# Block-sparse attention with an MLP on one Trainium2 core: the row of maxima written by ScalarE in twelve heads, and one pair of heads fewer multiplied in whole fp32

## The chip, the cores and the metric

The kernel runs on one core of one Trainium2 chip. The metric is the device time of one execution in microseconds (us), the median of three runs. The engines are named as in the profile: PE is TensorE's matmul and PEld its weight load, DVE is VectorE, ACT is ScalarE, POOL is GpSimd, SP is SyncE, which here only issues DMAs.

## What is computed

Four batches of eight heads, 768 positions, head dimension 64. Scores are masked by blocks of 32 (neighbours, first and last block, and three drawn blocks for each row of blocks), and an MLP with a piecewise activation follows on the joined heads:

```python
scores = scale * np.matmul(q, k.transpose(0, 1, 3, 2))
scores = np.where(mask, scores, -1000000000.0)
scores = scores - np.max(scores, axis=-1, keepdims=True)
attn = np.exp(scores)
attn = attn / (np.sum(attn, axis=-1, keepdims=True) + 1e-09)
attn_out = np.matmul(attn, v)
...
h = x @ w_in
g = np.where(pos, h, np.where(neg, 0.0, (h + beta) ** 2 / (4.0 * beta)))
return (g @ w_out).astype(np.float32)
```

## The kernel before

**Accuracy by splitting.** Most matmuls run in the type F32R. To keep fp32 accuracy an operand is split into a rounded part and a remainder, and products of the parts are added up. Queries and keys of a head lie in QA and KA (rounded parts, rows 0 to 63, and below them the mask rows 64 to 95) and in QB and KB (remainders beside rounded parts). There are two sets of QA and KA, used by heads in turn (SETS is 2).

**A head**, `head` (L198), works in this order. Twelve matmuls `max_mm` (L267) give the masked scores by rows, and twelve DVE reductions `max_red` (L272) their row maxima. `max_col` (L276) joins the two halves of each maximum into the tile mr, 128 x 6. `max_turn` (L280) transposes mr on PE into 6 x 128 in a PSUM bank. `max_row` (L283), on DVE, multiplies it by a constant of minus ones on a diagonal and so writes six rows of QA, 96 to 101; the keys have six rows of ones there, so that the matmul of the scores subtracts the maximum. Then, for each of two halves of the queries and six blocks of keys, `scores` (L303, L304: two F32R matmuls of 384 columns), `expo` (L308, ACT), and `values` (L333 to L336).

**Whole and split heads.** For the pairs of heads in WHOLE, which are heads 0 to 9, `values` is one fp32 matmul with the exponentials as they are (L333); ones beside the values give the row sums, and `o_whole` (L351, L353) copies both out on ACT. For all other heads ACT rounds each exponential (`p_hi`, the helper's line L196), DVE subtracts (`p_lo`, L316), PE multiplies twice (L335, L336), POOL adds the exponentials up (`p_sum`, L323), DVE reduces that sum (L358), adds two halves of the output (L345, after a copy by ACT on L340), and splits the values of the head (L243). A small matmul (L363) and L369 give the sums of a pair.

**Wide heads.** Heads 0 to 7 (batch 0) have no MLP work beside them; they may use the MLP's PSUM banks for scores, and the three `pa` banks are left to the maxima. From head 8 on, the scores, the maxima and the transposed maxima all share the three `pa` banks, and the MLP of the batch before (`moe`, L434: L457 to L459, L463 to L478, L485 to L487) runs between the heads' steps. Its first half, beside heads 8 to 11, also makes the two parts of w_out out of float64 bits (`convert`, L157; DVE lines L169 to L180, ACT L168 and L196). The same is done with w_in beside heads 0 to 7.

**Order.** Each step is put on a list with a due time (`at`, L129) worked out from the constants P, PW (wide heads) and PA (heads 8 to 15); the list is sorted and given to the framework, which puts in the waits. An engine works through its own instructions in order. None of these due times is touched by the change. All DMAs but one small kind are issued by SP.

Of the kernel before, what the change touches and what calls it, by code (L numbers as in the profile page):

```python
# [9 lines left out]
F32R = mybir.dt.float32r  # L10
# [10 lines left out]
T = 6  # L21
HALF = 384
# [15 lines left out]
def body(ctx, tc, qk_t, v, sampled_blocks, moe_w_in, moe_w_out, ind, cm, negd, ident, fold, out):  # L38
    nc = tc.nc
# [8 lines left out]
    pr = pool("pr", 1)  # L48
# [24 lines left out]
    def f(ap):  # L73
        return ap.bitcast(F32)


    idr = cst.tile([128, 128], F32R, name="idr")
# [4 lines left out]
    QA = [cst.tile([128, S], F32R, name=f"QA{i}") for i in range(SETS)]  # L82
# [4 lines left out]
    def consts():  # L87
        M = slice(64, KM)
        for i in range(SETS):
            nc.gpsimd.memset(f(QA[i][64:128 if i == 0 else 96]), 0.0)  # L90
        nc.gpsimd.memset(VW[0][:, :, 64:128], 1.0)
        nc.gpsimd.memset(VW[1][:, :, 0:64], 1.0)
        nc.vector.memset(eps, 1e-9)
        nc.vector.memset(half_c, 0.5)
        sraw = cst.tile([128, NR, 2], I32, name="sraw")
        nc.sync.dma_start(out=sraw[M], in_=sampled_blocks.bitcast(I32).rearrange("a (r w) -> a r w", w=2))
        cmt = cst.tile([128, 2 * NB], F32, name="cmt")
        nc.sync.dma_start(out=cmt[M], in_=cm)
        ef = f(cv.tile([128, 512, 2], I32, name="raw", bufs=3).rearrange("p c w -> p (c w)"))[64:KA, 0:S]
        nc.sync.dma_start(out=ef, in_=ind)  # L100
        idf = pp.tile([128, HALF], F32, name="pt")[:, 0:128]
        nc.sync.dma_start(out=idf, in_=ident)
        nc.vector.tensor_copy(out=idr, in_=idf)
        nc.vector.tensor_copy(out=KAt[0][64:KA], in_=ef)
        nc.sync.dma_start(out=nd, in_=negd.rearrange("a (t p) -> a t p", t=T))
        nc.sync.dma_start(out=sel, in_=fold)
        for i in range(1, SETS):
            rounded(nc.gpsimd, KAt[i][64:KA], ef)
        sf = cst.tile([128, NR], F32, name="sf")
        nc.vector.tensor_copy(out=sf[M], in_=sraw[M, :, 0])  # L110
        al = cst.tile([128, NB], F32, name="al")
        nc.vector.tensor_copy(out=al[M], in_=cmt[M, 0:NB])
        for r in range(NR):
            nc.vector.scalar_tensor_tensor(
                out=al[M], in0=cmt[M, NB:2 * NB], scalar=sf[M, r:r + 1], in1=al[M],
                op0=ALU.is_equal, op1=ALU.max)
        mb = cst.tile([128, NB], F32R, name="mb")
        nc.vector.tensor_scalar(out=mb[M], in0=al[M], scalar1=-1.0, scalar2=BIG, op0=ALU.add, op1=ALU.mult)
        for hf in range(2):
            cs = slice(hf * HALF, (hf + 1) * HALF)  # L120
            pm = psa.tile([128, 512], F32, name="pa")
            nc.tensor.matmul(out=pm[0:NB, 0:HALF], lhsT=mb[M], rhs=KAt[0][64:KM, cs], start=True, stop=True)
            for i in range(SETS):
                (nc.scalar.copy if i else nc.vector.tensor_copy)(out=QA[i][64:KM, cs], in_=pm[0:NB, 0:HALF])
# [4 lines left out]
    def at(t, fn, *args):  # L129
        plan.append((t, fn, args))  # L130
# [3 lines left out]
    def bank(wide, use="s"):  # L134

        if wide:
            ring = RINGS[use]
            n = turns[use] = turns.get(use, -1) + 1
            name = ring[n % len(ring)]
            if name[0] == "o":  # L140
                return psc.tile([128, DM], F32, name=name)
            if name == "hp":
                return psh.tile([128, 512], F32, name="hp")
        return psa.tile([128, 512], F32, name="pa")
# [45 lines left out]
    def rounded(eng, dst, src):  # L190
        if eng is nc.vector:
            eng.tensor_copy(out=dst, in_=src)
        elif eng is nc.gpsimd:
            eng.tensor_scalar(out=dst, in0=src, scalar1=1.0, scalar2=0.0, op0=ALU.mult, op1=ALU.add)
        else:
            eng.copy(out=dst, in_=src)  # L196

    def head(i, n0, b, h, pst):  # L198

        j, e = divmod(h, 2)  # L200
        wide = i < H
        whole = i // 2 in WHOLE
        G = {**P, **PW} if wide else {**P, **PA} if i < 2 * H else P
        o0, o1 = (L, R) if e == 0 else (R, L)
        QAi, KAi = QA[i % SETS], KAt[i % SETS]
        st = {}
# [67 lines left out]
        def max_col(lo=0, n=T):  # L274
            mr = st["mr"] = pr.tile([128, T], F32R, name="mr", bufs=2)
            nc.vector.tensor_tensor(out=mr[:, 0:n], in0=st["mc"][:, 0:n, 0], in1=st["mc"][:, 0:n, 1], op=ALU.max)  # L276

        def max_turn(lo=0, n=T):
            pm = st["pr"] = bank(wide, "m")
            nc.tensor.transpose(out=pm[0:n, 0:128].bitcast(F32R), in_=st["mr"][:, 0:n], identity=idr)  # L280

        def max_row(lo=0, n=T):
            nc.vector.tensor_tensor(out=QAi[96:96 + n].rearrange("a (t p) -> a t p", t=T)[:, lo:n],  # L283
                                    in0=st["pr"][0:n, 0:128].unsqueeze(1).to_broadcast([n, n - lo, 128]),
                                    in1=nd[0:n, lo:n], op=ALU.mult)
# [6 lines left out]
        if i == 0:  # L292
            for d, fn in ((-0.9, max_col), (-0.89, max_turn), (-0.88, max_row)):
                at(pre - (G["m0"] - G["m1"] / 2) + G["mr"] + H0 + d, fn, 0, T // 2)
        at(pre - G["mc"], max_col, T // 2 if i == 0 else 0)
        at(pre - G["mt"], max_turn, T // 2 if i == 0 else 0)
        at(pre - G["mw"], max_row, T // 2 if i == 0 else 0)


# [98 lines left out]
        for hf in range(2):  # L398
# [19 lines left out]
            if e:  # L418
# [6 lines left out]
                y -= G["r1"]  # L425
                y += G["r2"] + (XLATE if wide and j < NP - 1 else 0)
                at(y + G["xm"], x_mul, hf)
# [98 lines left out]


    at(TC, consts)
    for i in range(NHEADS):
        b, h = divmod(i, H)  # L530
        if h % 2 == 0:
            pst = {}
        head(i, PER * i, b, h, pst)
# [17 lines left out]
        fn(*args)  # L551


WHOLE = (0, 1, 2, 3, 4)
P = {'vw': 4.0, 'r1': 0.857, 'r2': 4.031, 'qs': 9.647, 'ks': 11.666, 'vs': 9.131, 'ld': 5, 'm0': 7.832, 'm1': 5.0, 'mr': 0.46, 'mc': 2.3, 'mt': 1.325, 'mw': 0.9, 'ex': 0.524, 'ph': 1.22, 'pl': 1.349, 'ps': 0.841, 'ow': 0.704, 'ot': 0.2, 'oa': 0.549, 'ah': 0.3, 'al': 0.578, 'su': 0.637, 'de': 1.414, 'yw': 0.799, 'yy': 2.173, 'xm': 0.774, 'xh': 1.0, 'xl': 2.518, 'gr': 0.1, 'gs': 0.279, 'gm': 0.314, 'gh': 0.934, 'gl': 1.232, 'l2': 1.494, 'l3': 0.158, 'l1': 0.121, 'cl': 9.0, 'cs': 1.705, 'cd': 1.8, 'co': 5.196, 'lag': 3.5}
PW = {'vw': 4.0, 'r1': 3.302, 'r2': 4.413, 'qs': 12.454, 'vs': 9.131, 'ld': 5, 'm0': 7.8, 'm1': 5.61, 'mr': 0.15, 'mc': 2.3, 'mt': 1.3, 'mw': 0.9, 'ex': 0.2, 'ph': 1.231, 'pl': 1.349, 'ps': 0.841, 'ow': 0.722, 'ot': 0.2, 'oa': 0.462, 'ah': 0.3, 'al': 0.578, 'su': 0.637, 'de': 1.525, 'yw': 0.813, 'yy': 2.024, 'xm': 0.516, 'xh': 1.1600000000000001, 'xl': 2.268, 'lag': 3.403}
TC = -90
XLATE = 2.0
H0 = 0.711
PH1 = ()  # L560
# [67 lines left out]
```

## Time and profile before

| | us |
|---|---|
| median of 3 runs | 982.35 (981.95 to 989.32) |
| the profiled execution, its own time | 983.67 |
| its span, first to last instruction | 981.8 |
| PE busy | 942.5 |
| DVE busy | 747.5 |
| ACT busy | 636.5 |
| POOL busy | 251.8 |

The profiled execution's own time is 1.9 us over its span, and 1.3 us over the median. The first exponential (L308) of head 8 starts at 151.1 us, that of head 10 at 206.1 and that of head 12 at 274.4, so that the stretch 17 to 151 is heads 0 to 7, 151 to 206 is heads 8 and 9, and 206 to 274 is heads 10 and 11. In a row of groups the two numbers behind the first bar are busy us and mean ns of one instruction; behind the second bar is the idle time of the engine just before them and what ended most of it. Durations of successive instructions overlap a little, so that a group's sum may exceed what it adds to the engine's busy time.

### The profile page before, as it was taken

To read this page: it belongs to the slowest core of one execution; us is meant where nothing else is said; L and a number is where in the kernel's file an instruction comes from. 1 tells how busy PE (TensorE), PEld (TensorE's weight loads), DVE (VectorE), ACT (ScalarE), POOL (GpSimd) and SP (SyncE) were. 2 spreads that over 40 slices of the span, in tenths; PEclk is the share of its full clock that TensorE was granted. 3 is DMA by queue.
4 is the path that set the end of the run, shared out by engine and by line. 5 is a ranking of instruction groups with operands and counts; after the bars stand their busy time and mean duration, and the time that the engine had idled before them with its cause. 6 is when DMAs were issued, how large, how long until landed. Compare 5 with 4: busy or idle time off the path is not lost.

```text
span 981.8 us, 14556 instructions
## 1 busy us (share of the span) xinstructions
PE 942.5 (96%) x4687; PEld 828.1 (84%) x4687; DVE 747.5 (76%) x1403; ACT 636.5 (65%) x1302; POOL 251.8 (26%) x229
## 2 busy tenths in 40 slices
PE   5899899999889999999999999999999999999998
PEld 3666677877779899999989998998999999899997
DVE  5888999889998888978788888888888885422222
ACT  3667777677667676767677767776767676433433
POOL 1000000023334343433434343343434343000000
PEclk9999999999999999999999999999999999999999
DMA  6756677754355444645555443645445432433432
GB/s 195 205 149 189 196 209 225 259 180 139 123 182 163 145 143 133 182 139 153 159 150 182 131 150 116 199 137 175 138 142 178 125 115 89 154 130 129 160 129 97
DMA packets 56216, 154.43 MB, mean 157 GB/s; under 512 B 9612, under 2 KB 17952, under 8 KB 56140
## 3 DMA queue, kind: packets, MB, share of 16 engines
q1 hardware_dynamic: 56100, 153.48, 51.5%
q8 instruction: 37, 0.61, 0.3%
q14 instruction: 39, 0.32, 0.1%
q10 hardware_dynamic: 40, 0.03, 0.0%
HBM read 100.92 MB, written 14.81 MB: 118 GB/s over the span
## 4 chain that ended last, share of the span: by engine, by line
PE 85%; DVE 7%; ACT 3%; DMA 2%; issue 2%; SPq 0%; ACTq 0%; DVEq 0%
PE oa L485 8%; PE oa L487 8%; PE oa L486 8%; PE hp L457 8%; PE hp L459 7%; PE hp L458 7%; PE pa L267 7%; PE pa L303 5%; PE pa L304 5%; PE po L335 5%; PE po L336 4%; PE po L333 4%; DVE mc L272 2%; PE oa L333 2%; DMA QA<-qkh 1%
## 5 line engine op out<-in xcount | busy, mean ns | idle before, releaser
L323 POOL TENSOR_TENSOR acc<-acc,pt 128x384 f32<-128x384 f32 x176 | 201.7, 1146 | 233.0 <-ACT pt L308 195.1
L272 DVE TENSOR_REDUCE mc<-pa 128x1 f32<-128x384 f32 x384 | 202.5, 547 | 19.3 <-PE pa L267 16.1
L196 ACT CAST ph<-pt 128x384 fp32r<-128x384 f32 x264 | 135.5, 514 | 92.4 <-PE po L335 89.3
L316 DVE TENSOR_TENSOR pl<-pt,ph 128x384 fp32r<-128x384 f32 x264 | 163.6, 620 | 34.7 <-ACT ph L196 34.0
L308 ACT ACTIVATE pt<-pa 128x384 f32<-128x384 f32 x288 | 140.6, 489 | 54.6 <-PE pa L304 45.0
L457 PE MATMUL hp<-x,wi 128*128 128x384 f32 x448 | 155.5, 347 | 4.0 <-DVE r L469 4.0
L485 PE MATMUL oa<-w,gh 128*128 128x512 f32 x384 | 153.3, 399 | 0.3 <-ACT gh L196 0.3
L487 PE MATMUL oa<-w,gl 128*128 128x512 f32 x384 | 151.6, 395 | 0.3 <-DVE gl L478 0.3
L459 PE MATMUL hp<-x,wi 128*128 128x384 f32 x448 | 151.2, 338 | 0.0
L458 PE MATMUL hp<-x,wi 128*128 128x384 f32 x448 | 151.1, 337 | 0.0
L486 PE MATMUL oa<-w,gh 128*128 128x512 f32 x384 | 150.8, 393 | 0.0
L267 PE MATMUL pa<-KA,QA 88*128 88x384 f32 x384 | 138.3, 380 | 5.4 <-DMA QA<-qkh 3.8
L323 POOL TENSOR_TENSOR acc<-pt 128x384 f32<-128x384 f32 x44 | 46.5, 1058 | 345.5 <-ACT pt L308 345.5
L469 DVE SCALAR_TENSOR_TENSOR r<-r,hp 128x384 f32<-128x384 f32 x112 | 61.5, 549 | 73.3 <-ACT r L466 72.9
L478 DVE TENSOR_TENSOR gl<-r,gh 128x384 fp32r<-128x384 f32 x128 | 84.3, 658 | 24.0 <-ACT gh L196 23.5
L303 PE MATMUL pa<-QA,KA 102*128 102x384 f32 x288 | 99.0, 344 | 1.8 <-ACT pt L308 1.1
L463 ACT ACTIVATE r<-hp,half_c 128x384 f32<-128x384 f32 x112 | 65.1, 582 | 54.1 <-PE hp L459 51.2
L304 PE MATMUL pa<-QB,KB 128*128 128x384 f32 x288 | 97.9, 340 | 0.0
L267 PEld LDWEIGHTS pa<-KA,QA 88*128 88x128 f32 x384 | 73.1, 192 | 28.7 <-DVE mc L272 4.7
L335 PE MATMUL po<-ph,vn 128*128 128x384 f32 x264 | 91.4, 346 | 5.1 <-DVE xun L345 3.4
L457 PEld LDWEIGHTS hp<-x,wi 128*128 128x128 f32 x448 | 84.5, 189 | 10.7 <-DVE r L469 6.1
L336 PE MATMUL po<-pl,vn 128*128 128x384 f32 x264 | 88.6, 336 | 0.0
(97 smaller groups left out, 1624.3 us busy)
## 6 DMA issues: line engine op xcount, KB each, us to landing
w<-wo_dram SPq DMA_DIRECT2D x112, 512.0 KB
qk<-in_qk_t_dram SPq DMA_DIRECT2D x32, 384.0 KB
raw<-in_moe_w_in_dram SPq DMA_DIRECT2D x16, 512.0 KB
raw<-in_moe_w_out_dram SPq DMA_DIRECT2D x16, 512.0 KB
wo_dram<-w SPq DMA_DIRECT2D x16, 512.0 KB
lv<-in_v_dram SPq DMA_DIRECT2D x32, 192.0 KB
KA<-qkh SPq DMA_DIRECT2D x32, 192.0 KB
QA<-qkh SPq DMA_DIRECT2D x32, 192.0 KB
```

Of the source, the lines that this page charges most:

```text
L267: nc.tensor.matmul(out=pm[:, 0:HALF], lhsT=QAi[0:KM, t * 128:(t + 1) * 128], rhs=KAi[0:KM, kh * HALF:(kh + 1) * HALF], start=True, stop=True)
L272: nc.vector.reduce_max(out=st["mc"][:, t, kh:kh + 1], in_=st.pop(("pm", t, kh))[:, 0:HALF], axis=AX.X)
L303: nc.tensor.matmul(out=ps[:, 0:HALF], lhsT=KAi[0:KA, ks], rhs=QAi[0:KA, cs], start=True, stop=False)
L304: nc.tensor.matmul(out=ps[:, 0:HALF], lhsT=st["KB"][:, ks], rhs=st["QB"][:, cs], start=False, stop=True)
L316: (nc.gpsimd if i < 2 * H and c in PL1 else nc.vector).tensor_tensor(out=pl, in0=st["p", c], in1=f(st["ph", c]), op=ALU.subtract)
L323: nc.gpsimd.tensor_tensor(out=st["acc", hf], in0=prev, in1=st["p", c], op=ALU.add)
L457: nc.tensor.matmul(out=hv, lhsT=wi[:, j, 0, fs], rhs=x[:, 0], start=(j == 0), stop=False)
L458: nc.tensor.matmul(out=hv, lhsT=wi[:, j, 0, fs], rhs=x[:, 1], start=False, stop=False)
L459: nc.tensor.matmul(out=hv, lhsT=wi[:, j, 1, fs], rhs=x[:, 0], start=False, stop=(j == NP - 1))
L485: nc.tensor.matmul(out=o, lhsT=gh[:, ts], rhs=w[:, 0], start=(fi == 0), stop=False)
L486: nc.tensor.matmul(out=o, lhsT=gh[:, ts], rhs=w[:, 1], start=False, stop=False)
L487: nc.tensor.matmul(out=o, lhsT=gl[:, ts], rhs=w[:, 0], start=False, stop=(fi == NF - 1))
```

## The change

Heads 0 to 11 (ONE) write one row of maxima in place of six: six transposes of one column each go to row 0 of two PSUM banks, 3 x 128 columns in each, and two ACT instructions copy 384 columns each, times minus one, into row 96 of QA. Rows 97 to 101 stay zero, which the memset now does for both sets. Heads 12 and later keep the old way. WHOLE loses its last pair, so that heads 8 and 9 are split as the later ones are.

```diff
@@ consts
-            nc.gpsimd.memset(f(QA[i][64:128 if i == 0 else 96]), 0.0)
+            nc.gpsimd.memset(f(QA[i][64:128]), 0.0)
@@ head
+        def max_turn_one(lo=0, n=T):
+            for hf in range(lo // 3, n // 3):
+                pm = st["pr", hf] = bank(wide, "m")
+                for k in range(3):
+                    nc.tensor.transpose(out=pm[0:1, k * 128:(k + 1) * 128].bitcast(F32R),
+                                        in_=st["mr"][:, 3 * hf + k:3 * hf + k + 1], identity=idr)
+
+        def max_row_one(lo=0, n=T):
+            for hf in range(lo // 3, n // 3):
+                nc.scalar.mul(out=QAi[96:97, hf * HALF:(hf + 1) * HALF], in_=st["pr", hf][0:1, 0:HALF], mul=-1.0)
+
         def max_turn(lo=0, n=T):
+            if i < ONE:
+                return max_turn_one(lo, n)
             pm = st["pr"] = bank(wide, "m")
...
         def max_row(lo=0, n=T):
+            if i < ONE:
+                return max_row_one(lo, n)
...
-WHOLE = (0, 1, 2, 3, 4)
+WHOLE = (0, 1, 2, 3)
...
+ONE = 12
```

## Rows read from the trace of the kernel before

**Rows 1.** The page: PE's share, PE in 40 slices, the granted clock.
```profile
PE 942.5 (96%) x4687; PEld 828.1 (84%) x4687; DVE 747.5 (76%) x1403; ACT 636.5 (65%) x1302; POOL 251.8 (26%) x229
...
PE   5899899999889999999999999999999999999998
...
PEclk9999999999999999999999999999999999999999
```
**Rows 2.** Busy time by stretch: length; PE, PEld, DVE, ACT, POOL; clock, DMA share, GB/s.
```profile
17.00:151.00 134.00, 124.53 (x504) 91.47 (x504) 117.92 (x233) 92.37 (x185) 0.00 (x0) 0.99 0.65 189
151.00:206.00 55.00, 54.43 (x249) 44.03 (x249) 48.05 (x94) 37.35 (x74) 0.00 (x0) 1.00 0.73 233
206.00:274.00 68.00, 60.83 (x296) 50.70 (x295) 63.65 (x109) 45.74 (x95) 23.82 (x20) 1.00 0.45 145
274.00:305.00 31.00, 28.35 (x148) 25.48 (x148) 30.04 (x56) 22.03 (x48) 11.67 (x10) 1.00 0.60 187
389.00:417.00 28.00, 28.00 (x150) 25.93 (x149) 24.65 (x47) 21.49 (x46) 12.08 (x10) 1.00 0.65 186
```
**Rows 3.** Chain of waits, 151 to 275: start, us, what.
```profile
152.27 0.65 PE po L333 x2
...
162.39 0.52 PE pa L267 x3
```
**Rows 4.** Groups of DVE instructions, 206 to 274 (heads 10 and 11).
```profile
L316 DVE TENSOR_TENSOR pl<-pt,ph 128x384 fp32r<-128x384 f32 x23 | 16.2, 703 | 0.4 <-ACT ph L196 0.4
...
L478 DVE TENSOR_TENSOR gl<-r,gh 128x384 fp32r<-128x384 f32 x7 | 5.5, 785 | 2.9 <-ACT gh L196 2.9
...
L174 DVE SCALAR_TENSOR_TENSOR cva<-raw,cva 128x512 int32<-128x512 int32 x5 | 4.5, 909 | 0.0
...
L387 DVE TENSOR_TENSOR xun<-xun,den 128x384 f32<-128x384 f32 x2 | 2.1, 1042 | 0.6 <-DMA den<-s 0.6
...
L358 DVE TRANSPOSE_TENSOR_REDUCE psum<-acc 128x12 f32<-128x384 f32 x3 | 1.7, 562 | 0.0
L345 DVE TENSOR_TENSOR xun<-po,otmp 64x384 f32<-64x384 f32 x3 | 1.6, 546 | 0.0
```
**Rows 5.** The largest split group of DVE in the steady part, 389 to 445.
```profile
L316 DVE TENSOR_TENSOR pl<-pt,ph 128x384 fp32r<-128x384 f32 x24 | 14.7, 613 | 2.7 <-ACT ph L196 2.6
```
**Rows 6.** Groups of DVE instructions, 151 to 206 (heads 8 and 9).
```profile
L174 DVE SCALAR_TENSOR_TENSOR cva<-raw,cva 128x512 int32<-128x512 int32 x9 | 6.2, 688 | 0.1
...
L478 DVE TENSOR_TENSOR gl<-r,gh 128x384 fp32r<-128x384 f32 x7 | 3.9, 551 | 2.0 <-ACT gh L196 2.0
...
L283 DVE TENSOR_TENSOR QA<-pa,nd 6x768 fp32r<-6x768 f32 x2 | 1.9, 950 | 0.9 <-PE pa L280 0.8
...
L387 DVE TENSOR_TENSOR xun<-xun,den 128x384 f32<-128x384 f32 x2 | 1.1, 548 | 0.0
```
**Rows 7.** Timeline of POOL and of DVE near 219.
```profile
219.21 1.01 POOL L323 TENSOR_TENSOR acc<-acc,pt 128x384 f32<-128x384 f32 x1 [1.53 <-ACT pt L308]
...
218.96 0.54 DVE L272 TENSOR_REDUCE mc<-pa 128x1 f32<-128x384 f32 x1
219.43 1.21 DVE L316 TENSOR_TENSOR pl<-pt,ph 128x384 fp32r<-128x384 f32 x1
```
**Rows 8.** Waits, 17 to 151: us in total, times, longest.
```profile
PE oa L303 <- DVE QA L283: 5.2, 7, 1.2
```
**Rows 9.** Groups of the whole span, shapes kept apart.
```profile
L280 PE MATMUL pa<-idr,mr 128*6 128x128 f32 x32 | 9.5, 297 | 2.5 <-DVE mr L276 2.5
...
L351 ACT ACTIVATE den<-po,eps 1x384 f32<-1x384 f32 x12 | 6.9, 573 | 1.1 <-PE po L333 1.0
...
L280 PEld LDWEIGHTS pa<-idr,mr 128*6 128x6 f32 x32 | 2.7, 84 | 4.6 <-DVE mr L276 2.4 <-issue 1.1
```
**Rows 10.** Timeline, 84 to 90 (all engines) and 115 to 122 (ACT).
```profile
85.87 0.57 ACT L351 ACTIVATE den<-oa,eps 1x384 f32<-1x384 f32 x1 [1.67 <-PE oa L333]
...
117.31 0.62 ACT L196 CAST wi<-cva 128x512 fp32r<-128x512 f32 x1
117.95 0.57 ACT L351 ACTIVATE den<-oa,eps 1x384 f32<-1x384 f32 x1
118.54 0.83 ACT L196 CAST qkh<-qk 128x768 fp32r<-128x768 f32 x1
```

## Prediction

> **What bounds the kernel now.** I read the page's shares and slices first. PE is busy 96% of the span, and its granted clock is at 90% or more of the upper of its two levels in every slice [rows 1], 0.99 to 1.00 by stretch [rows 2]; so the clock plays no part here and PE sets the time on the whole. But that share is a mean over stages, so next I cut the span at the heads and read busy time by stretch in the same view. Four stages appear. In the steady part, shown by 28 us of it, PE is busy all the time and DVE 24.65 of 28. In heads 8 and 9 (55 us) PE is still full, 54.43, and DVE has 7 us to spare, 48.05; POOL does nothing. In heads 10 and 11 (68 us) the order turns: DVE 63.65, PE only 60.83. In head 12 (31 us) DVE is at 30.04. So there is one place, from about 206 to 305 us, in which DVE and not PE sets the pace: there each head carries both the work of a split head and the conversion of w_out. Heads 0 to 7 (134 us) lie between, PE 124.53 and DVE 117.92: both nearly full, taking turns in waiting.
>
> The change takes 0.95 us of DVE out of each of heads 0 to 11 and puts a split head's DVE work into heads 8 and 9, just ahead of the stretch that has no DVE time left. That is the core of the case.
>
> **Part one: heads 8 and 9 are split.** PE's side gains. One whole multiplication takes two passes, 0.65 us together [rows 3]. Three F32R matmuls of 384 columns take 0.52 us, so one takes 0.173 and the two that replace a whole one 0.35. Twenty-four times 0.65 minus 0.35 is 7.2 us of PE work less in a stretch in which PE is full.
>
> DVE's side loses, term by term for the two heads:
> - 24 subtractions for the remainder, at 0.613 us as in the steady part [rows 5] or 0.703 as in heads 10 and 11 [rows 4]: 14.7 to 16.9 us.
> - 4 reductions of the summed exponentials at 0.562 and 4 additions of output halves at 0.546 [rows 4]: 4.4 us.
> - The split of the values, of which one of two falls into the stretch, and the small additions for the sums of the pair: no more than 1 us, by the size of the rows around.
> - Successive DVE instructions overlap: a reduction of 0.54 us starts at 218.96 and the next instruction at 219.43, 0.47 later [rows 7]. On some 33 added instructions that takes 0.07 each off, 2.3 us.
>
> So 17.8 to 20 us are added. Two `max_row` leave, 1.9 us [rows 6]. With 48.05 before [rows 2] the stretch then holds 64 to 66 us of DVE work, where it had 55 us of time.
>
> POOL's additions come along: 20 of them run in heads 10 and 11, none in heads 8 and 9 [rows 2], and 20 will. In the one stretch against the other the same DVE instructions are slower beside POOL: the remainder of g 0.785 against 0.551, the joining of bits 0.909 against 0.688, the scaling of x 1.042 against 0.548 [rows 4, 6]. For the 7, 9 and 2 of them in heads 8 and 9 that is 1.6, 2.0 and 1.0, together 4.6 us at most, and 0 at least. I take half, which gives 67 to 68 us of work.
>
> How it comes about is seen in one pair of rows: an addition on POOL runs from 219.21 to 220.22, and a DVE subtraction that starts at 219.43 lasts 1.21 us, until 220.64, which is 0.42 after POOL's end [rows 7]. The Trainium skill, SBUF — State Buffer, section "Who interferes with whom", has the rule behind it, and it speaks against this change: a DVE instruction with two inputs in SBUF and a GpSimd instruction that reads SBUF use one port pair, and the second to start waits until the first has finished. By that rule, the trace agrees for this pair; the means above show that most instructions miss each other. Its worst case is the third rival below.
>
> A stretch is never filled to the last. DVE was busy 63.65 of 68 us (94%) in heads 10 and 11 and 30.04 of 31 (97%) in head 12 [rows 2]. So heads 8 and 9 take between 64 / 0.97 = 66 and 70.6 / 0.94 = 75 us; I take 68 / 0.96 = 71, that is 16 more than now, with ends at 11 and 20. A second way agrees: two split heads with conversions take 68 us now [rows 2], and heads 8 and 9 carry more of the conversion (9 joinings against 5 [rows 4, 6]), so 68 to 72, or 13 to 17 more. PE's 7.2 us are hidden whole: PE would have 48 us of work in 71.
>
> Can later stretches make it good? No: PE's order is fixed, heads 10 to 12 are DVE-bound themselves, and from there on PE has no idle time to give back.
>
> In heads 10 and 11 two more `max_row` leave a DVE-bound stretch: 1.9 / 0.94, 2 us less. Sum of heads 8 to 11: +14 (+9 to +18).
>
> **Part two: the row of maxima on ACT, heads 0 to 7.** Before the first score of heads 1 to 7 PE stands idle until DVE has written the six rows: seven waits, 5.2 us in all, the longest 1.2 [rows 8]. After it, one half of the scores needs only three transposes and one ACT copy. The nearest row to that copy is another ACT instruction with one partition and 384 columns, 0.573 us [rows 9], against 0.95 on DVE; the two copies of a head cost ACT 1.15 us. Where ACT is idle then (1.67 us ahead of 85.87 [rows 10]) the first score comes some 0.3 to 1 us earlier. Where ACT is in a row of work (a cast, a copy of sums and the cast of the next head's queries and keys from 117.31 to 119.37 [rows 10]) the copies push that row back by up to 1.15 us; queued behind them are the exponentials, and for those the score banks and then PE wait. By PE the five added transposes are 0.08 each, the time of their weight loads [rows 9]: 0.4 us a head, partly in a stretch in which PE waits anyway. And DVE, at 117.92 of 134, is freed of eight times 0.95 us, 7.6.
>
> Bounds for the eight heads: at best all 5.2 us of waits go and a little of DVE's relief shows, -7; at worst the ACT copies and the transposes stand in the path in most heads, (1.15 + 0.4) x 8 = 12 less half of the waits and of the relief, some +6. I take -2: gain and loss change from head to head, and DVE's relief tips it.
>
> A second bank of the three is held for a moment in heads 8 to 11; PE is not the bound there, so nothing is put down for it. The larger memset comes before anything waits on POOL: nothing.
>
> **Sum.** Against the profiled execution: 983.67 + 14 - 2 = 995.7. That execution is 1.3 us over the median of the runs, so the forecast is 994.5 us, 1.2% slower.
>
> **The rivals.**
> 1. *The stretch grows by its lower end and the wide heads gain at theirs.* DVE work of 64 us at 97%, little hindered by POOL, +11 - 2, and -6 in heads 0 to 7: +3, 985.5. For it: DVE's 7.6 us freed in heads in which DVE is 88% busy. Against it: ACT is then queued ahead of the exponentials. Within 1%.
> 2. *Faster: PE stays the bound in heads 8 and 9.* PE is full there now; if DVE's new work fits, the 7.2 us come off, and with -3 in the wide heads and -2 in heads 10 and 11 the time is 970. Its condition is that DVE work in that stretch stays below 48 us, the new PE need; it was 48.05 before anything is added, so some 17 us would have to move elsewhere. It decides once more than 10 us of the whole change are gained.
> 3. *Slower still: blocking by POOL in full.* Each of the 20 additions (1.01 us alone [rows 7]) holds up DVE for its whole length, 20 in place of the 2.3 that I put down, or (66 + 20) / 0.96 = 90 us for the stretch, +35; with -2 and -2 the time is some 1013. For it: the pair of rows above. Against it: in the means only 0.1 to 0.5 us are lost on each instruction. A milder form, with the ACT copies at their worst end, gives 1003.
>
> **How the numbers follow.** About 1% (9.8 us) is what can be told from no change here, so "same" ends at 992.2, inside my own spread. Forecast (988 to 1002) 0.62, first rival (below 988) 0.18, second 0.08, third 0.12. From the forecast's own 0.62 I put 0.13 below 992.2. So faster 0.08, same 0.31, slower 0.61. The range from 983 to 1006 takes in the bounds +9 - 7 and +18 + 6 with the 1.3 off, and leaves out the second rival and the far end of the third.
>
> **What would show it.** In the profile after: DVE at 93% or more, PE at 70 to 75%, in heads 8 and 9, which last 68 to 74 us from the first exponential of head 8 to that of head 10; POOL busy there for 20 additions; heads 10 and 11 at about 66; the steady part untouched at 28 a head. In heads 0 to 7 the waits on L283 are gone, a wait of the first score on an ACT instruction of 0.5 to 0.6 us stands in their place, and the stretch is 134 less 2, between 127 and 140. The forecast is wrong if heads 8 and 9 stay below 62 us, or if the wide heads gain more than 7.

## The result, and the profile after

The changed kernel took 992.25 us (median of 6 runs, 990.16 to 993.45), the kernel before 983.18 in the runs beside it (the two medians are 9.1 us apart). Over all these runs it is 1.0083 times as long, with a 95% interval of 1.0065 to 1.01. That is 8.2 us slower (6.4 to 9.8): less than 1%, but the interval lies clear of no change. The profiled execution took 991.48 us with a span of 989.5; against 983.67 before that is 7.8 more.

The page of the changed kernel, to be laid beside [rows 1]:
```profile
PE 944.8 (95%) x4750; PEld 833.4 (84%) x4750; DVE 760.7 (77%) x1426; ACT 652.5 (66%) x1346; POOL 276.1 (28%) x249
...
PE   5898998889989999999999999999999999999998
```
PE's busy time hardly moved (942.5 to 944.8), although 24 whole multiplications became cheaper (by 7.2 us in the prediction's sum). Against that, some sixty transposes came with the row, and a lower clock, shown below, lengthened other matmuls. The transposes of one column, to be read beside the first line of [rows 9], where 32 of six columns took 9.5 us and 12 have left:
```profile
L282 PE MATMUL pa<-idr,mr 128*1 128x128 f32 x72 | 8.2, 248 | 4.0 <-DVE mr L276 4.0
```
In the slices PE stands at 8 from the seventh to the ninth, where it stood at 9 before: heads 8 and 9.

Busy time by stretch, columns as in [rows 2]. Head 8 now starts at 152.1 us, head 10 at 214.0, head 12 at 284.8:
```profile
17.00:152.00 135.00, 126.07 (x542) 93.15 (x540) 114.69 (x232) 99.42 (x204) 0.00 (x0) 0.99 0.67 193
152.00:214.00 62.00, 52.99 (x261) 44.82 (x260) 59.41 (x105) 43.50 (x94) 22.17 (x20) 0.97 0.52 169
214.00:285.00 71.00, 63.46 (x309) 53.43 (x308) 69.56 (x125) 47.74 (x100) 26.25 (x20) 0.98 0.49 163
285.00:315.00 30.00, 27.37 (x143) 24.51 (x142) 29.08 (x53) 21.42 (x48) 11.67 (x10) 1.00 0.60 187
427.00:455.00 28.00, 28.00 (x148) 25.62 (x147) 22.35 (x43) 19.20 (x41) 10.39 (x11) 1.00 0.46 139
```
In heads 8 and 9 the roles of PE and DVE have changed over: before, PE was busy 54.43 of 55 and DVE 48.05; now DVE 59.41 of 62 and PE 52.99. Heads 10 and 11, bound by DVE before, are more so: 69.56 of 71. Between first exponentials the stretches compare as follows (us):

| heads | before | after | difference | predicted |
|---|---|---|---|---|
| 0 to 7 | 133.6 | 134.6 | +1.1 | -2 |
| 8 and 9 | 55.0 | 62.0 | +7.0 | +16 |
| 10 and 11 | 68.3 | 70.8 | +2.5 | -2 |
| 12 | 30.2 | 30.2 | 0 | 0 |
| 13 to the end | 677.3 | 674.5 | -2.8 | 0 |

The last row is no work of the change. From head 12 on every engine has the same instructions in the same order in both kernels; a few heads there take up to 28.8 us in place of 27.8, other ones in each execution, and over the profiles read here this part lies between 672 and 678. One profiled execution, that of the kernel with the mixed copies and heads 10 and 11 whole, was slow (2697.25 us) and is not read.

DVE's groups in heads 8 and 9 after (152 to 214), which answer to [rows 4, 6]:
```profile
L331 DVE TENSOR_TENSOR pl<-pt,ph 128x384 fp32r<-128x384 f32 x23 | 16.1, 702 | 0.9 <-ACT ph L196 0.9
...
L174 DVE SCALAR_TENSOR_TENSOR cva<-raw,cva 128x512 int32<-128x512 int32 x5 | 4.2, 832 | 0.0
L484 DVE SCALAR_TENSOR_TENSOR r<-r,hp 128x384 f32<-128x384 f32 x7 | 3.8, 549 | 0.9 <-ACT r L481 0.8
L493 DVE TENSOR_TENSOR gl<-r,gh 128x384 fp32r<-128x384 f32 x6 | 3.8, 638 | 0.0
```
The 24 subtractions are there, at the dearer of the two prices. But only 5 joinings of bits are left in this stretch where there were 9 [rows 6]: of the conversion of w_out some was done earlier and some later. The earlier part shows in DVE's groups of 130 to 152, ahead of head 8:
```profile
L180 DVE TENSOR_TENSOR w<-cva,w 128x512 fp32r<-128x512 f32 x2 | 1.4, 685 | 0.0
```
Two of the sixteen parts of w_out are finished there; before the change none was. In heads 8 and 9 five are finished in place of eight, in heads 10 and 11 eight in place of seven.

### The profile page after: what moved, and what is told of

It is laid out like the page before. It is cut to its first block, busy times and chain, and to the rows that moved or that the text cites. A ratio compares the mean times of both kernels' runs of the same rounds, so it can differ in the third digit from the quotient of the medians.

```text
span 989.5 us, 14802 instructions
## 1 busy us (share of the span) xinstructions
PE 944.8 (95%) x4750; PEld 833.4 (84%) x4750; DVE 760.7 (77%) x1426; ACT 652.5 (66%) x1346; POOL 276.1 (28%) x249
## 4 chain that ended last, share of the span: by engine, by line
PE 82%; DVE 10%; DMA 4%; ACT 2%; issue 2%; SPq 0%; DVEq 0%; ACTq 0%
PE oa L500 8%; PE oa L502 8%; PE oa L501 8%; PE hp L472 7%; PE hp L473 7%; PE hp L474 7%; PE pa L267 6%; PE po L350 5%; PE pa L318 5%; PE pa L319 4%; PE po L351 4%; PE po L348 3%; PE oa L348 3%; DVE mc L272 2%; DVE pl L331 2%
## 5 line engine op out<-in xcount | busy, mean ns | idle before, releaser
L338 POOL TENSOR_TENSOR acc<-acc,pt 128x384 f32<-128x384 f32 x192 | 222.4, 1158 | 264.9 <-ACT pt L323 215.4
L196 ACT CAST ph<-pt 128x384 fp32r<-128x384 f32 x288 | 147.6, 514 | 90.6 <-PE po L350 87.2
L331 DVE TENSOR_TENSOR pl<-pt,ph 128x384 fp32r<-128x384 f32 x288 | 180.6, 627 | 34.0 <-ACT ph L196 33.1
L338 POOL TENSOR_TENSOR acc<-pt 128x384 f32<-128x384 f32 x48 | 50.2, 1046 | 297.6 <-ACT pt L323 297.6
L350 PE MATMUL po<-ph,vn 128*128 128x384 f32 x288 | 100.3, 348 | 4.1 <-DVE xun L360 4.1
L351 PE MATMUL po<-pl,vn 128*128 128x384 f32 x288 | 97.6, 339 | 1.6 <-DVE pl L331 1.5
```

Of the source, the lines that this page charges most:

```text
L331: (nc.gpsimd if i < 2 * H and c in PL1 else nc.vector).tensor_tensor(out=pl, in0=st["p", c], in1=f(st["ph", c]), op=ALU.subtract)
L338: nc.gpsimd.tensor_tensor(out=st["acc", hf], in0=prev, in1=st["p", c], op=ALU.add)
L350: nc.tensor.matmul(out=po, lhsT=st["vn"][:, c], rhs=st["ph", c], start=(c == 0), stop=False)
```

## The experiments

The diffs are against the changed kernel, except where another is named. Ratios are to the kernel before, run beside each on the same chip; lengths of stretches are from first exponential to first exponential in the one profiled execution.

**Each part alone.** First the row alone:
```diff
-WHOLE = (0, 1, 2, 3)
+WHOLE = (0, 1, 2, 3, 4)
```


> Only the row of maxima goes to ScalarE in heads 0 to 11; heads 8 and 9 stay whole. Theory A (the cost of the change is the split pair's DVE work in a stretch that DVE bounds; the row by ScalarE is about neutral in heads 0 to 7 and saves its DVE time in heads 10 and 11): 979 to 983 us, -1 to -4 against the kernel before, heads 10 and 11 some 2 us shorter than 68.3. Rival B (the row by ScalarE costs time of its own, by two instructions of ScalarE ahead of the exponentials and five transposes): 985 us or more, heads 0 to 7 at least 2 us longer than 133.6.

Measured: 0.9974 (0.9957 to 0.9991), 979.93 us. Its stretches of heads 0 to 7, 8 and 9, and 10 and 11:
```profile
17.00:154.00 137.00, 126.95 (x540) 93.97 (x538) 114.81 (x232) 99.68 (x205) 0.00 (x0) 0.98 0.66 191
154.00:210.00 56.00, 55.69 (x265) 45.92 (x266) 43.22 (x85) 38.59 (x76) 0.00 (x0) 1.00 0.68 223
210.00:274.00 64.00, 58.73 (x297) 50.53 (x295) 62.47 (x109) 45.56 (x96) 23.32 (x20) 1.00 0.43 141
```
Theory A holds for the total and for heads 10 and 11 (64.7 between first exponentials, -3.6). Heads 0 to 7 took 136.4, the rival's sign; whether that is the row's price is settled two groups below.

Then the split alone, with the six rows left to DVE:
```diff
-            nc.gpsimd.memset(f(QA[i][64:128]), 0.0)
+            nc.gpsimd.memset(f(QA[i][64:128 if i == 0 else 96]), 0.0)
...
-ONE = 12
+ONE = 0
```


> Only heads 8 and 9 are split; the row of maxima stays on DVE. Theory A: the stretch of heads 8 to 11 is longer than in the changed kernel by the four rows of 0.95 us that stay on DVE, 132.8 + 3.8 = 136 to 137 us, and the time is 993 to 997. Rival B (the row is what costs): the time is below 989, and heads 8 to 11 take 131 us or less.

Measured: 1.0211 (1.019 to 1.0233), 1002.37 us, above theory A's range; heads 8 to 11 took 143.0, not 137. So the split is what costs. Theory A fell short because it counted the rows alone. Heads 8 and 9, then 10 and 11, and the parts of w_out finished in the four heads, here and in the changed kernel:
```profile
149.00:219.00 70.00, 60.44 (x262) 50.03 (x262) 66.25 (x117) 44.71 (x93) 23.01 (x20) 0.88 0.50 163
219.00:292.00 73.00, 63.49 (x293) 52.52 (x292) 71.91 (x128) 47.74 (x97) 24.48 (x20) 0.95 0.51 161
```
```profile
L180 DVE TENSOR_TENSOR w<-cva,w 128x512 fp32r<-128x512 f32 x15 | 10.8, 721 | 0.5 <-ACT w L196 0.5
```
```profile
L180 DVE TENSOR_TENSOR w<-cva,w 128x512 fp32r<-128x512 f32 x13 | 9.9, 764 | 0.0
```
With the six rows on DVE in heads 0 to 7 too, no part of w_out is finished ahead of head 8. DVE is busy for 138.2 us of heads 8 to 11 (128.7 in the changed kernel), 97% of their time in both kernels, so that its work accounts for the longer stretch; heads 0 to 7 took 2.1 us less (132.5). Something else came with it, at the start of head 8:
```profile
149.00:155.00 6.00, 4.53 (x22) 3.26 (x21) 5.79 (x9) 4.50 (x11) 3.47 (x4) 1.00 0.72 190
155.00:168.00 13.00, 10.37 (x30) 8.47 (x29) 10.93 (x21) 7.17 (x16) 3.35 (x3) 0.53 0.39 138
```
PE was busy 4.53 of 6 us, and its longest waits at that point, of 1.3 and 1.4 us, were for DVE's subtraction (L331); then its granted clock fell to the lower of its two levels (1.2 for 2.4 GHz; 0.53 in the mean of the second row) for 13.7 us. The changed kernel has the same in small, with one such wait of 1.5 us:
```profile
155.00:158.00 3.00, 1.47 (x8) 1.04 (x7) 2.89 (x4) 1.80 (x5) 1.78 (x3) 1.00 0.75 196
158.00:162.00 4.00, 3.70 (x13) 3.27 (x12) 4.00 (x8) 1.99 (x5) 1.91 (x2) 0.57 0.74 218
```

**Is it DVE, and is it POOL beside it?** Two kernels leave work out in heads 8 and 9. One drops the 24 subtractions:
```diff
-            nc.tensor.matmul(out=po, lhsT=st["vn"][:, c], rhs=st["pl", c], start=False, stop=(c == T - 1))
+            nc.tensor.matmul(out=po, lhsT=st["vn"][:, c], rhs=st["pl" if i not in (8, 9) else "ph", c], start=False, stop=(c == T - 1))
...
-                    at(s + G["pl"], p_lo, c)
+                    if i not in (8, 9):
+                        at(s + G["pl"], p_lo, c)
```


> The changed kernel, but heads 8 and 9 leave out the 24 DVE subtractions for the remainder of the exponentials; the second multiplication takes the rounded part once more, so that PE's work is the same. Theory A (DVE bounds heads 8 to 11): some 15 us of DVE work leave, and heads 8 to 11 fall from 132.8 us to between 118 and 123, bounded then by PE; the time is 977 to 983. Rival C (PE waits there for the exponentials and their rounding by ScalarE, or for PSUM banks): heads 8 to 11 stay at 128 us or more, the time at 987 or more.

Measured: 0.9969 (0.9951 to 0.9987), 979.3 us; heads 8 to 11 took 120.0 us, 12.8 less than in the changed kernel. Heads 8 and 9, then 10 and 11:
```profile
154.00:209.00 55.00, 51.86 (x264) 44.41 (x265) 50.26 (x91) 44.36 (x96) 23.61 (x20) 1.00 0.66 212
209.00:273.00 64.00, 59.54 (x296) 53.53 (x295) 60.98 (x112) 45.71 (x96) 26.94 (x20) 0.95 0.49 156
```
Theory A is right in both its numbers, rival C is out: without the subtractions the split costs nothing against the row alone (979.93). DVE's work sets this stretch.

The other cuts POOL's additions from 20 to 4:
```diff
         def p_sum(hf, c):
+            if i in (8, 9) and c > 1:
+                return
```


> The changed kernel, but GpSimd adds up only the first two blocks of exponentials of each half in heads 8 and 9: 4 additions in place of 20, the row sums of these heads are then incomplete. Everything else stays. If an addition holds up DVE by 0.1 to 0.25 us in the mean, heads 8 to 11 get 2 to 4 us shorter (time 987 to 990); if it holds DVE up by its whole length, 10 us or more shorter (982 or less); if it holds up nothing that counts, less than 1 us.

Measured: 1.0012 (0.9997 to 1.0027), 983.36 us, 0.71% or 7 us less than the changed kernel, between two of the cases. Heads 8 to 11 shrank from 132.8 to 122.0, and DVE's busy time in them from 128.7 to 119.4 although DVE does the same work, 227 instructions of the same kinds: 9.3 us on 16 additions, 0.58 each, from one profiled execution of each kernel. (Head 12 took 2.8 us more, with 6.8 us at the lower clock.) DVE's groups in heads 8 to 11, first of the changed kernel (152 to 285), then without the additions (152 to 274):
```profile
L172 DVE SCALAR_TENSOR_TENSOR cva<-raw,cva 128x512 int32<-128x512 int32 x12 | 11.8, 982 | 0.0
...
L402 DVE TENSOR_TENSOR xun<-xun,den 128x384 f32<-128x384 f32 x4 | 3.0, 744 | 0.0
```
```profile
L172 DVE SCALAR_TENSOR_TENSOR cva<-raw,cva 128x512 int32<-128x512 int32 x12 | 9.3, 778 | 0.1
...
L404 DVE TENSOR_TENSOR xun<-xun,den 128x384 f32<-128x384 f32 x4 | 2.2, 547 | 0.0
```
The same instruction falls from 982 to 778 ns, and another from 744 to 547. In the mean an addition takes DVE 0.58 of its 1.0 us. That is less than its whole length, the worst case that the third rival takes from the rule in the Trainium skill, SBUF — State Buffer, section "Who interferes with whom", and more than twice what I had put down.

**The row in heads 0 to 7.** In the first of these kernels heads 0 to 7 keep the six rows by DVE and ScalarE writes the row in heads 8 to 11 alone:
```diff
-            nc.gpsimd.memset(f(QA[i][64:128]), 0.0)
+            nc.gpsimd.memset(f(QA[i][64:128 if i == 0 else 96]), 0.0)
...
-            if i < ONE:
+            if 8 <= i < ONE:
...
-            if i < ONE:
+            if 8 <= i < ONE:
...
+        if i in (8, 9):
+            at(pre - G["m0"] - 0.5, lambda: nc.gpsimd.memset(f(QAi[96:128]), 0.0))
...
-WHOLE = (0, 1, 2, 3)
+WHOLE = (0, 1, 2, 3, 4)
```


> The row by ScalarE in heads 8 to 11 alone, heads 0 to 9 whole; GpSimd, idle there, clears the rows 96 to 127 of either set once, ahead of heads 8 and 9. Theory E (the row by ScalarE costs heads 0 to 7 about 2 us and pays in heads 8 to 11): heads 0 to 7 back at 132 to 134 us, the time 976 to 980, at or below the kernel with the row in all twelve. Rival D (DVE's relief in heads 0 to 7 is carried through its queue and spent in heads 8 to 11, so that it is needed there): 980 to 983.

Measured: 0.9971 (0.9959 to 0.9982), 980.54 us; that is the row in all twelve heads (0.9974) within the interval. Heads 0 to 7 took 135.0. So theory E is not borne out: in heads 0 to 7 the row by ScalarE neither gains nor costs anything that can be measured. The time falls in rival D's range, but its mechanism is not borne out either, since the relief in heads 0 to 7 is missing here and the time is the same. The gain of 3 us comes with the row in heads 8 to 11; the one profiled execution shows 1.1 of it there (122.2 against 123.3), and the row in all twelve heads 2.8 (120.5).

The second keeps the one row and its transposes, but DVE copies it:
```diff
-                nc.scalar.mul(out=QAi[96:97, hf * HALF:(hf + 1) * HALF], in_=st["pr", hf][0:1, 0:HALF], mul=-1.0)
+                nc.vector.tensor_single_scalar(out=QAi[96:97, hf * HALF:(hf + 1) * HALF],
+                                               in_=st["pr", hf][0:1, 0:HALF], scalar=-1.0, op=ALU.mult)
...
-WHOLE = (0, 1, 2, 3)
+WHOLE = (0, 1, 2, 3, 4)
```


> As the kernel with the row alone (heads 0 to 9 whole), but the two copies of the one row are made by DVE: the six transposes and two banks stay, ScalarE gets nothing. If the copies in ScalarE's queue are what costs heads 0 to 7 their 2 us: these are back at 132 to 134 us. If the transposes and the second bank are: 135 us or more. DVE's work is about that of the kernel before (two copies of 0.45 to 0.5 us for one of 0.95), so the time is 981 to 984 in the first case and 984 to 987 in the second.

Measured: 0.994 (0.9921 to 0.9958), 976.64 us, better than either case; heads 0 to 7 took 128.7 us against 133.6 before. The transposes and the second bank show no cost there. The copies (engine, then ns as minimum/median/maximum), first by ScalarE in the kernel with the row alone, then by DVE:
```profile
L287 ACT ACTIVATE QA<-pa x24: 461/478/482, 15.2 to 236.8; 1x384 fp32r<-1x384 f32 x24
```
```profile
L287 DVE TENSOR_SCALAR QA<-pa x24: 539/550/553, 15.0 to 230.4; 1x384 fp32r<-1x384 f32 x24
```
DVE's copy is the slower instruction, and its kernel the faster one. What PE waited for ahead of the first scores says why in part; waits of heads 0 to 7, of the kernel before, of the changed kernel and of the one with DVE's copies, to be read beside [rows 8]:
```profile
PE pa L267 <- DMA QA<-qkh: 1.2, 1, 1.2
```
```profile
PE oa L318 <- ACT QA L287: 3.4, 4, 1.2
...
PE pa L267 <- DMA QA<-qkh: 2.0, 2, 1.3
```
```profile
PE oa L318 <- DVE QA L287: 2.1, 3, 0.9
...
PE pa L267 <- DMA QA<-qkh: 0.8, 1, 0.8
```
The wait of 5.2 us fell to 3.4 by ScalarE, but there PE waited longer for the next head's queries (2.0 against 1.2). At one head it is seen how: their cast stands behind the copies on ScalarE (a copy at 86.05, the cast at 86.53, the exponentials from 87.28). By DVE the wait fell to 2.1: the first half of the scores waits for 0.55 us of DVE in place of 0.95, and ScalarE's queue stays as it was. These two waits are 2.5 us of the 5.9 by which heads 0 to 7 differ between the changed kernel and this one; all of PE's idle time there is 8.9 us in the one and 5.1 in the other (9.5 before). The Trainium skill, ScalarE: Activation LUTs, section "Rules for kernel authors", says to give a multiplication to VectorE and not to ScalarE, on the ground of DVE's rate per element in bf16; in heads 0 to 7 the runs agree with the advice but not with the ground, for this row in fp32 takes DVE 550 ns and ScalarE 478.

**Where the four rows of heads 8 to 11 count.** The split with the row by ScalarE in heads 0 to 7 only:
```diff
-ONE = 12
+ONE = 8
```


> The changed kernel (heads 8 and 9 split) with the row by ScalarE in heads 0 to 7 only. Theory D (what DVE is spared in heads 0 to 7 moves through its queue and shortens the bound stretch behind): four rows of 0.95 us more on DVE than in the changed kernel, 994 to 998 us. Rival (only what DVE is spared within heads 8 to 11 counts): as with no row by ScalarE at all, 1000 to 1003.

Measured: 1.0201 (1.0184 to 1.0217), 1003.12 us, as without any row by ScalarE, which is what its rival expected. Four DVE instructions of 0.95 us in heads 8 to 11 cost 11.6 us once heads 8 and 9 are split (1.0201 less 1.0083), and 3 us while these are whole. To part their load from their place, the same load without the place:
```diff
+            if i >= 8:
+                d = pr.tile([128, 2, HALF], F32R, name="dummy", bufs=2)
+                nc.vector.tensor_tensor(
+                    out=d[0:1], in0=st["pr", 1][0:1, 0:HALF].unsqueeze(1).to_broadcast([1, 2, HALF]),
+                    in1=nd[0:1].rearrange("a t p -> a (t p)").rearrange("a (h p) -> a h p", h=2), op=ALU.mult)
```


> The changed kernel with four DVE instructions more: in heads 8 to 11 DVE makes one product of the size and place of the old row (0.95 us, after the same transposes), which nobody reads; the scores go on taking the row of ScalarE. The kernel with the old row in these four heads was 10.9 us slower than the changed one, for 3.8 us of DVE work. Theory L (DVE's load alone does it: what DVE is late by makes PE idle, and more is lost than the load): 999 to 1003 us. Theory P (it is the place in the chain: the scores wait for a row that stands behind DVE's backlog): 994 to 997, the load of 3.8 us at most.

Measured: 1.014 (1.0118 to 1.0162), 995.65 us, in theory P's range. The load of 3.8 us costs 5.6, some 3 either way by the two intervals, and so about half of the 11.6. What the other half is, is not shown. Theory P puts it on the scores, which wait for a row behind DVE's backlog; but with the old row in heads 8 to 11 PE waited for that row (L298) only 0.6 us, and far longer for a DVE instruction of the MLP. Waits, 152 to 293:
```profile
PE hp L472 <- DVE r L484: 7.9, 5, 2.4
...
PE pa L318 <- DVE QA L298: 0.6, 2, 0.4
```
In the changed kernel these two are 3.7 and 0.3 us. Nor does the experiment part load and place cleanly, since the product that nobody reads also holds one of the three `pa` banks until DVE has made it. Heads 8 and 9, then 10 and 11, first with the old row, then with the load alone:
```profile
152.00:219.00 67.00, 58.79 (x260) 49.04 (x260) 61.60 (x107) 42.48 (x89) 23.75 (x20) 0.90 0.48 153
219.00:293.00 74.00, 64.78 (x299) 53.59 (x298) 72.44 (x130) 48.32 (x99) 23.26 (x20) 0.95 0.51 162
```
```profile
154.00:216.00 62.00, 53.98 (x265) 45.28 (x264) 59.42 (x104) 44.24 (x93) 25.04 (x20) 0.97 0.52 163
216.00:288.00 72.00, 66.03 (x306) 54.01 (x305) 70.80 (x130) 48.86 (x100) 26.98 (x20) 0.95 0.52 166
```
The clock goes with the length (0.90 against 0.97 in heads 8 and 9); which of the two causes the other is left open below. In the profiled execution with the load (998.18 us) heads 8 to 11 took only 0.8 us more than in the changed kernel; heads 0 to 7 took 1.9 more, and head 12 took 2.8 more, with 6.8 us at the lower clock.

**Towards a better kernel.** Heads 10 and 11 whole as well:
```diff
-WHOLE = (0, 1, 2, 3)
+WHOLE = (0, 1, 2, 3, 4, 5)
```


> The changed kernel with heads 0 to 11 whole: four heads more by one fp32 multiplication than in the changed kernel. Theory A (DVE bounds heads 8 to 11): DVE in heads 10 and 11 loses some 20 us of work, PE gains 7.2; these two heads become bound by PE at 63 to 66 us against 64.7 with the row alone, head 12 falls from 30.1 to about 28, and the time is 976 to 981. Rival (PE's extra 7 us show in full): 985 or more.

Measured: 0.9956 (0.9939 to 0.9973), 977.95 us. Heads 10 and 11:
```profile
207.00:270.00 63.00, 62.94 (x296) 51.93 (x294) 43.82 (x83) 39.88 (x77) 0.00 (x0) 1.00 0.51 158
```
They are bound by PE now (62.94 of 63) with DVE at 43.82, as theory A had it; head 12 did not get shorter (30.1).

The row copied by DVE in heads 0 to 7 and by ScalarE in 8 to 11, heads 0 to 9 whole:
```diff
-                nc.scalar.mul(out=QAi[96:97, hf * HALF:(hf + 1) * HALF], in_=st["pr", hf][0:1, 0:HALF], mul=-1.0)
+                if wide:
+                    nc.vector.tensor_single_scalar(out=QAi[96:97, hf * HALF:(hf + 1) * HALF],
+                                                   in_=st["pr", hf][0:1, 0:HALF], scalar=-1.0, op=ALU.mult)
+                else:
+                    nc.scalar.mul(out=QAi[96:97, hf * HALF:(hf + 1) * HALF], in_=st["pr", hf][0:1, 0:HALF], mul=-1.0)
...
-WHOLE = (0, 1, 2, 3)
+WHOLE = (0, 1, 2, 3, 4)
```


> Heads 0 to 9 whole as before, one row of maxima in heads 0 to 11, copied by DVE in heads 0 to 7 and by ScalarE in heads 8 to 11. If the two findings add up (copies by DVE bring heads 0 to 7 to 129 us; without the row on DVE heads 10 and 11 take 64.7 us in place of 68.3): 972 to 976 us, below every kernel so far. If they don't, because what is gained in heads 0 to 7 was the transfers' place in that one order: 977 to 981.

Measured: 0.9943 (0.9924 to 0.9963), 976.88 us, just above the first range, and the same as with all copies by DVE (0.994): in heads 8 to 11 it makes no measurable difference, while heads 8 and 9 are whole, which of the two engines copies the row. Heads 0 to 7 came down to 128.2 and heads 8 to 11 to 121.7, but head 12 took 31.6 and the rest happened to be 678.3.

The same, with heads 10 and 11 whole too (against the mixed kernel):
```diff
-WHOLE = (0, 1, 2, 3, 4)
+WHOLE = (0, 1, 2, 3, 4, 5)
```

> The kernel with the mixed copies, heads 10 and 11 whole too. Theory A (DVE bounds these heads, PE has time to spare there): 1 to 3 us below the mixed kernel, 970 to 974. Rival: no difference or slower, if PE's 7.2 us more show.

Measured: 0.993 (0.9913 to 0.9948), 976.07 us, above theory A's range: 0.8 us below the mixed kernel, as its rival had it. It is the lowest ratio, but not told apart from the mixed kernel (0.9943) and the one with all copies by DVE (0.994). These three beat both given kernels, by 0.6 to 0.7% against the kernel before.

Last, the mixed row with the split of the change (against the mixed kernel):
```diff
-WHOLE = (0, 1, 2, 3, 4)
+WHOLE = (0, 1, 2, 3)
```


> The changed kernel (heads 8 and 9 split) with the one row copied by DVE in heads 0 to 7 and by ScalarE in heads 8 to 11. If the time that the copies by DVE win in heads 0 to 7 (about 6 us against copies by ScalarE) is passed on whole, through the stretch that DVE bounds: 985 to 988 us, 9 to 11 above the mixed kernel with whole heads. If DVE's extra load of 7 us in heads 0 to 7 is handed on to that stretch as backlog: 990 to 995, no better than the changed kernel.

Measured: 1.0099 (1.0081 to 1.0118), 993.81 us, in the range of the second case. What DVE's copies win in heads 0 to 7 (129.6 us, 5 less than in the changed kernel) is lost again in heads 8 to 11 (140.1, 7.3 more). No part of w_out was finished ahead of head 8 here, where the changed kernel had two; and after PE had been busy 3.23 of 5 us its clock fell for longer, 10.2 us in place of 3.4:
```profile
150.00:155.00 5.00, 3.23 (x14) 1.95 (x12) 5.00 (x8) 3.48 (x8) 2.61 (x4) 1.00 0.73 196
155.00:166.00 11.00, 10.59 (x30) 8.26 (x31) 9.31 (x18) 6.72 (x15) 2.88 (x3) 0.53 0.38 120
```

## Why the prediction was right, and where it was off

*The core was right.* The split moves the load of heads 8 and 9 from PE to DVE, PE's saving does not show, and the time grows. The kernels with one part each (the row alone 0.9974, the split alone 1.0211), and the one without the subtractions (0.9969), show this.

*DVE's work over heads 8 to 11* was predicted to grow by 16.3 to 18.5 us (17.8 to 20 added, 2.3 for POOL, 3.8 of rows gone). It grew by 16.7, from 112.0 to 128.7 busy. But the agreement is luck, since errors offset each other. POOL's additions cost more, 0.58 us each, near 12 us for 20; my terms held some 5 (the 2.3, and what lies above 0.55, the median of a subtraction, in the prices of 0.613 to 0.703). Against that, two conversions of w_out had left the stretch, near 6 us. And only three rows left it, 2.9 us in place of 3.8: those of heads 9, 10 and 11. That of head 8 stands ahead of its first exponential, and that of head 12, which falls into heads 10 and 11, stays on DVE.

*Where it fell was wrong.* I gave heads 8 and 9 a fixed amount, 67 to 68 us, and so 71 us of time; they hold 59.4 and take 62.0, below my lower bound of 66; unrounded it is 61.98, which is even just under the 62 that I had named as a sign that the forecast is wrong. PE was busy for 85% of it, not 70 to 75. Heads 10 and 11 were to shrink by 2 and grew by 2.5. The step that failed is the one that treated a stretch of DVE's queue as closed: the conversion has slack of several us to either side, and it went to where DVE had time. So the time of each stretch was wrong, while the sum over heads 8 to 11 held, by the errors named above.

*The fill was off by a little.* I took 94 to 96%; over heads 8 to 11 DVE reached 97%. DVE's work and the fill together make +9.5 for the stretch in place of +14, at the low end of +9 to +18. The profiled execution took 4.2 us less than the 995.7 forecast for it: 4.5 less in heads 8 to 11, 2.8 less from head 13 on, which is no work of the change, and 3.1 more in heads 0 to 7. That the total came out so near is in part luck.

*The wide heads* were put at -2 (-7 to +6) and measured +1.1. The trade was seen rightly, shorter waits for the row against a longer queue on ScalarE; DVE's relief there buys no time in heads 0 to 7 (114.3 us busy in place of 117.5), it buys conversions done early. In total these win nothing: the split with the row by ScalarE in heads 0 to 7 finishes two parts early and takes 134.4 us for heads 0 to 7 and 140.9 for 8 to 11, the split alone none, 132.5 and 143.0.

*The rivals.* The first (985.5) and the second (970) did not come: DVE's new work does not fit, as its sum said. The third in full, +35 for heads 8 and 9, did not come either; its mechanism is real at 0.58 us for an addition in place of 1.01.

*What stays open.* The prediction had no term for the clock, which plays no part in heads 8 to 11 of the kernel before. The lower clock may be an effect of a starved PE and a cause of more time alike. Over heads 8 to 11 the time that the trace's clock record shows at the lower level goes with their length: 6.8 us of it in the changed kernel (132.8 us long), 10.2 with the extra load (133.6), 20.5 with the old row (140.9), 23.9 with the split alone (143.0) and with the mixed row (140.1). How much of the length it makes by itself was not tried. DVE's idle time in these heads gives a hint: 4.1 us in the changed kernel, 3.8 with the extra load, 4.8 with the split alone, so that there DVE's work is enough to explain the length; but 6.9 with the old row and 7.5 with the mixed row, so that there some 3 us may be the lower clock's.

## What to carry to other kernels

Before work is moved from one engine to another, add up the receiving engine's time over the whole run of stretches that its queue can shift work between, not over one stretch; and count what a third engine's new instructions do to the receiver's old ones. A row of a few values that a large matmul waits for did best, in heads 0 to 7, on the engine where it pushed back nothing else that PE waits for, in pieces that let the first half go; that this engine's instruction is the longer one (550 to 478 ns) mattered less.

## What was not expected of the hardware

The granted clock of PE fell to its lower level although PE's longest waits there were 1.5 us and less: for 3.4 us after it had been busy 1.47 of 3 us, for 13.7 us after 4.53 of 6. In the kernel before it stood at 1.00 throughout heads 8 to 11 [rows 2]. And an addition on GpSimd that runs beside a dense DVE queue took 0.58 us of DVE's time in the mean, shown by leaving 16 of them out.
